# Other ranks for small transfers, and tiny vector operations planned freely, in the opening of an attention and two-MoE kernel

## The chip, the cores and the metric

The kernel runs on one core of one Trainium2 chip. The metric is the device time of one execution in microseconds (us); a comparison uses the median over several executions.

## What is computed

The reference chains three layers over 4 batches of 576 tokens.

```python
scores = scale * q @ k.T                      # 4 batches, 8 heads, 576 x 576, head size 64
cum = cumsum(maximum(s, 0))
bias = minimum(-(cum[:, None] - cum[None, :]), 0)
attn = softmax(where(causal, -1e9, scores + bias))
x = (attn @ v), heads side by side            # 2304 tokens x 512
x = moe(x, w_gate, w_val, w_out, rms_g)       # root-mean-square norm, silu(g) * val, 512 -> 1536 -> 512
x = moe2(x, w2_gate, w2_val, w2_out)          # the same without the norm
```

## The kernel before

All work is given to a planner as operations. Each has an engine, an assumed duration, the buffers that it reads and writes, and a rank `pri`. `Plan.run` walks an assumed timeline: when an engine comes free, it takes the ready operation with the lowest rank. The result is a fixed order of instructions for each engine. On the chip each engine (PE for matmuls, DVE, ACT, POOL, and SP, which only issues transfers) works through its own order and stands still where the next instruction's data has not come.

Two more inputs of an operation matter here. `later` adds nanoseconds to the time at which the planner believes that an operation's forerunners on compute engines have released it. `port` says that a DVE operation must not be planned while a POOL operation runs: the planner then puts it after that operation (`if e == POOL or e == DVE and ops[n][7]` in `Plan.run`).

The opening works on the first 256 rows of batches 0 and 1, 16 early heads in all (`EarlyUnit`, called u0 to u15 here, in the order in which they are planned). Head u has rank u, its loads have u - 1000. For each head three transfers are issued in `EarlyUnit.load`:

- L879: q and k of the head, 128 KB, into a slot of `lq` (`lq_117` for even heads, `lq_121` for odd ones, two slots in each);
- L884: one row of the cumulated s, 1 KB, into row 64 of the same slot, from the fifth head on. Below it is called the s row;
- L891: v of the head, 64 KB, into a slot of `vl` (four slots as well). The first four heads take it from ACT's queue.

The score matmul (L899) needs q, k and the s row; the values matmul (L927) needs v and the exponentials, which come through DVE (L690), ACT (L701), a transpose on PE (L917) and a copy (L923 on DVE or L922 on ACT). A slot is free for head u + 4 when PE is done with head u.

The weights of the first MoE layer come beside this: 24 weight loads of 512 KB (L434, tile `raw`, ranks -992 and up in steps of 1.5 for two), each turned into two parts by L438 on ACT, L440 on DVE, L445 or L446 on ACT or POOL, and L449 on POOL or DVE. When the eight heads of a batch are done, `normalise` (called with `split=False` for the early heads) runs a chain of some 20 tiny DVE operations on 128x2 and 128x16 values (L1020 to L1054, written through `step`), then transposes (L1058), matmuls (L1066) and scalings (L1070), and with that the MoE matmuls (L1086) of the batch can start. They are queued behind the attention as work that fills PE's gaps; the hidden values that they give are stored by L1126. The loads of the later attention (L597, L599, L602, L605, L774) go through SP too.

Of the kernel before, what the change touches and what calls it, by code (L numbers as in the profile page):

```python
# [40 lines left out]
PE, DVE, ACT, POOL, SP, NONE = "PE", "DVE", "ACT", "POOL", "SP", "NONE"  # L41


def f32(ap):
    return ap.bitcast(F32)
# [34 lines left out]
class Plan:  # L80
# [20 lines left out]
    def op(self, eng, ns, fn, r=(), w=(), pri=0.0, later=0, port=False, slow=0.0):  # L101

        n = len(self.ops)
        done = 0
        if eng == SP:  # L110
            took = ns / self.RATE
            ns = max(450.0, took)
            done = 2300.0 + took - ns + slow
        deps, shared = set(), []
        for accesses, writes in ((r, False), (w, True)):
            for a in accesses:
                buf, part = a if isinstance(a, tuple) else (a, None)
                key = buf if isinstance(buf, str) else buf.key
                live = self.live.setdefault(key, [])
                keep = []  # L120
                for part2, m, wrote in live:
                    meets = part is None or part2 is None or part == part2
                    if meets and (writes or wrote) and m != n:
                        deps.add(m)
                    if not (writes and meets and (part is None or part == part2)):
                        keep.append((part2, m, wrote))
                keep.append((part, n, writes))
                self.live[key] = keep
                if not isinstance(buf, str) and buf.share is not None and buf not in shared:
                    shared.append(buf)  # L130
                    buf.uses += 1
        engs = eng if isinstance(eng, list) else [(eng, ns)]
        self.ops.append((engs, fn, deps, pri, done, shared, later, port))
        return n
# [160 lines left out]
TINY = 70  # L295
# [5 lines left out]
def tile_kernel(  # L301
# [16 lines left out]
    op = plan.op  # L318
# [10 lines left out]
    def buf(pool, tag, shape, dtype, name=None):  # L329
        return Buf(f"{pool}.{tag}",  # L330
                   lambda: pools[pool][1].tile(shape, dtype, name=name or tag, tag=tag))
# [143 lines left out]
    cumA = buf("at", "pTB1", [P, 2 * P], F32, "cumA")  # L475
# [100 lines left out]
    class Head:  # L576
# [13 lines left out]
        def load(self, pri):  # L590
            b, h, n, nv = self.b, self.h, self.n, self.nv
            i = b * NH + h
            c0 = self.c0
            q0, k0, c0_ = lq_parts(self.ql, 0)
            q1, k1, c1_ = lq_parts(self.ql, 1)
            self.qp, self.kp = [k0, k1], [q0, q1, c0_, c1_]
            op(SP, 4 * P * n, lambda en: en.dma_start(  # L597
                out=self.ql()[:, :n], in_=qk[b, h, :, 1, :n]), w=self.kp, pri=pri, later=2500)
            op(SP, 4 * D * (QW - c0), lambda en: en.dma_start(  # L599
                out=self.ql()[:D, S + c0:], in_=qk[b, h, :D, 0, c0:]),  # L600
               w=self.qp, pri=pri, later=2500)
            op(SP, 4 * P * n, lambda en: en.dma_start(  # L602
                out=self.cb()[:, :n], in_=cum_d[i:i + 1, :n].to_broadcast([P, n])),
               r=["cum_d"], w=[self.cb], pri=pri, later=2500)
            op(SP, 256 * P * nv, lambda en: en.dma_start(out=self.vl()[:, :nv], in_=vp[b, h, :, :nv]),  # L605
               w=[self.vl], pri=pri, later=2500)
# [241 lines left out]
    class EarlyUnit(Unit):  # L848
# [28 lines left out]
        def load(self, pri):  # L877
            ql, i = self.ql
            op(SP, 8 * D * 256, lambda en: en.dma_start(  # L879
                out=ql()[0:D, :, 288 * i:288 * i + 256], in_=qk[self.b, self.h, 0:D, :, 0:256]),  # L880
               w=self.parts[:2], pri=pri)
            n = self.b * NH + self.h
            if not self.first:
                op(SP, 1024, lambda en: en.dma_start(  # L884
                    out=ql()[D:D + 1, 1, 288 * i:288 * i + 256], in_=cumA()[n:n + 1]),
                   r=[cumA, self.rows], w=self.parts[2:], pri=pri, later=1000)
            if self.first:
                op(ACT, 450, lambda en: en.dma_start(
                    out=self.v(), in_=vp[self.b, self.h, :, 0:2]), w=[self.vl], pri=pri - 1e6)
            else:  # L890
                op(SP, 512 * P, lambda en: en.dma_start(  # L891
                    out=self.v(), in_=vp[self.b, self.h, :, 0:2]), w=[self.vl], pri=pri)

        def scores(self, pri):
            for t in self.tiles:
# [44 lines left out]
    def normalise(i, g, tot, pri, split=True):  # L940
# [15 lines left out]
        for k in range(KD):  # L956
# [3 lines left out]
               r=[(x, (k, 0)), (x, (k, 64))], w=[q], pri=pri)  # L960

            if not split:
                def sums(en, q=q, k=k):
# [9 lines left out]
                    out=qh()[:, :n], in0=q()[:, :n], scalar1=1.0, scalar2=1.0, op0=ALU.mult,  # L973
                    op1=ALU.mult)}, r=[q], w=[qh], pri=pri)
            op([(DVE, c_tt(n)), (POOL, c_ptt(n))], 0, lambda en, q=q, qh=qh: en.tensor_tensor(
                out=sqL()[:, :n], in0=q()[:, :n], in1=f32(qh()[:, :n]),
                op=ALU.subtract), r=[q, qh], w=[sqL], pri=pri, port=True)
# [6 lines left out]
        if split:  # L984
# [3 lines left out]
               r=[ps], w=[sq[0]], pri=pri)  # L988
            ps2 = mo_bank()
            for c in range(nt):  # L990
                op(PE, C_TR, lambda en, c=c: en.transpose(
                    ps2()[:, c * P:c * P + P], sq[0]()[:, at[c]:at[c] + P], ident()),
                   r=[sq[0], ident], w=[ps2], pri=pri)
# [3 lines left out]

        def step(fn, r=(), w=None):
            w = [col] if w is None else w
            op(DVE, TINY, fn, r=[*w, *r], w=w, pri=pri, port=True)  # L1000

        def m():
            return col()[:, 0, :nt]
# [10 lines left out]
        def over():  # L1014
            return fac()[:, 0, :nt]

        def u():
            return fac()[:, 1, :nt]
        F, U = (fac, 0), (fac, 1)
        step(lambda en: en.tensor_scalar(out=over(), in0=tot()[:, :nt], scalar1=1.0e-9,  # L1020
                                         scalar2=None, op0=ALU.add), [tot], [F])
        step(lambda en: en.reciprocal(over(), over()), [], [F])
        step(lambda en: en.tensor_tensor(out=u(), in0=squares(), in1=over(), op=ALU.mult),
             [ps, F], [U])
        step(lambda en: en.tensor_tensor(out=u(), in0=u(), in1=over(), op=ALU.mult), [F], [U])
        step(lambda en: en.tensor_reduce(out=m(), in_=u(), axis=mybir.AxisListType.X,
                                         op=ALU.add), [U])
# [6 lines left out]
        for _ in range(3):  # L1034
# [6 lines left out]
            out=over(), in0=over(),  # L1041
            in1=y().rearrange("p (t o) -> p t o", o=1).to_broadcast([P, nt, NH]),
            op=ALU.mult), [col], [F])
# [7 lines left out]
        def columns(z):  # L1051
# [3 lines left out]
                                         op=ALU.subtract), [F], [rr])  # L1055
        tp = mo_bank()
        for c in range(nt):
            op(PE, C_TR, lambda en, c=c: en.transpose(  # L1058
                tp()[:, at[c]:at[c] + P], rr()[:, c * P:c * P + P], ident()), r=[rr, ident], w=[tp],
               pri=pri)  # L1060
        op(ACT, c_act(n), lambda en: en.activation(rT(), tp()[:, :n], ACTF.Copy),
           r=[tp], w=[last], pri=pri)
        for k in range(KD):
# [7 lines left out]
                out=x()[:, k, :n], in0=x()[:, k, :n], scalar=gcol()[:, k:k + 1], in1=rs()[:, :n],  # L1071
                op0=ALU.mult, op1=ALU.mult), r=[rs, gcol], w=halves, pri=pri)
            op(ACT, c_act(n) + 35, lambda en, k=k: en.activation(H()[:, k, :n], x()[:, k, :n], ACTF.Copy),  # L1073
               r=halves, w=[(H, k)], pri=pri)
            op([(POOL, c_ptt(n)), (DVE, c_tt(n))], 0, lambda en, k=k: en.tensor_tensor(  # L1075
                out=L()[:, k, :n], in0=x()[:, k, :n], in1=f32(H()[:, k, :n]), op=ALU.subtract),
               r=halves + [(H, k)], w=[(L, k)], pri=pri, port=True)
# [56 lines left out]
    later = setup()  # L1134
# [767 lines left out]
```

## Time and profile before

| | |
|---|---|
| median of 3 runs | 1056.55 us (1052.65 to 1058.98) |
| the profiled execution, its own time | 1057.39 us |
| its span, first to last instruction | 1055.6 us |
| PE busy | 1040.2 us, 99% of the span |
| mean granted TensorE clock | 0.997 of full speed |

The span leaves out 1.79 us around the first and last instruction. Busy time of PE counts a matmul from its start to its modelled end, so neighbours overlap, and a PE that runs at half clock is as busy as one at full clock.

### The profile page before, as it was taken

To read this page: it belongs to the slowest core of one execution; us is meant where nothing else is said; L and a number is where in the kernel's file an instruction comes from. 1 tells how busy PE (TensorE), PEld (TensorE's weight loads), DVE (VectorE), ACT (ScalarE), POOL (GpSimd) and SP (SyncE) were. 2 spreads that over 40 slices of the span, in tenths; PEclk is the share of its full clock that TensorE was granted. 3 is DMA by queue.
4 is the path that set the end of the run, shared out by engine and by line. 5 is a ranking of instruction groups with operands and counts; after the bars stand their busy time and mean duration, and the time that the engine had idled before them with its cause. 6 is when DMAs were issued, how large, how long until landed. Compare 5 with 4: busy or idle time off the path is not lost.

```text
span 1055.6 us, 19496 instructions
## 1 busy us (share of the span) xinstructions
PE 1040.2 (99%) x6322; PEld 937.2 (89%) x6322; DVE 771.7 (73%) x1880; ACT 641.5 (61%) x1373; POOL 273.5 (26%) x370
## 2 busy tenths in 40 slices
PE   8899999999999999999999999999999999999998
PEld 6599999999999999999988889888888888888888
DVE  7699788777777776757779887665667766976462
ACT  6689778867664775333466865555556444665652
POOL 4368556544343542000000000212122221300000
PEclk9899999999999999999999999999999999999999
DMA  7797555534546732666697662666667667888673
GB/s 204 229 282 221 144 150 148 164 117 128 158 142 204 246 106 85 188 208 206 206 299 244 197 222 84 222 210 220 228 202 256 219 232 263 292 259 261 207 244 105
DMA packets 127959, 211.17 MB, mean 200 GB/s; under 512 B 16176, under 2 KB 55600, under 8 KB 127856
## 3 DMA queue, kind: packets, MB, share of 16 engines
q1 hardware_dynamic: 126656, 209.32, 62.8%
q8 instruction: 50, 0.82, 0.3%
q10 hardware_dynamic: 1200, 0.60, 0.2%
q14 instruction: 53, 0.43, 0.1%
HBM read 145.29 MB, written 64.56 MB: 199 GB/s over the span
## 4 chain that ended last, share of the span: by engine, by line
PE 79%; DMA 7%; DVE 6%; ACT 3%; issue 3%; POOL 1%; SPq 1%; ACTq 0%; POOLq 0%; DVEq 0%
PE mo L1086 21%; PE mo L1455 8%; PE mo L1626 8%; PE sps L1626 6%; PE tp L1455 6%; PE sps L1455 5%; PE tp L745 4%; PE tp L733 3%; PE sps L664 2%; PE mo L1702 2%; DMA raw<-in_w_gv 2%; PE sps L1086 2%; PE tp L1086 2%; PE mo L1510 2%; DMA lq<-cumA 1%
## 5 line engine op out<-in xcount | busy, mean ns | idle before, releaser
L1086 PE MATMUL mo<-xL,H 128*128 128x256 f32 (+1 forms) x672 | 201.8, 300 | 0.1
L1086 PE MATMUL mo<-xH,H 128*128 128x256 f32 (+1 forms) x672 | 200.7, 300 | 0.3
L1086 PE MATMUL mo<-xH,L 128*128 128x256 f32 (+1 forms) x672 | 200.2, 298 | 0.0
L1351 DVE TENSOR_TENSOR hL<-hh,hH 128x512 fp32r<-128x512 f32 (+1 forms) x192 | 125.2, 662 | 67.1 <-ACT hH L1348 66.4
L1348 ACT ACTIVATE hH<-hh 128x512 fp32r<-128x512 f32 (+1 forms) x192 | 115.2, 603 | 91.6 <-DVE hL L1351 21.3
L1086 PEld LDWEIGHTS mo<-xL,H 128*128 128x128 f32 x672 | 127.0, 189 | 1.0 <-POOL xL L1075 0.5
L1086 PEld LDWEIGHTS mo<-xH,H 128*128 128x128 f32 x672 | 126.7, 189 | 1.1 <-ACT xH L1073 0.6
L1086 PEld LDWEIGHTS mo<-xH,L 128*128 128x128 f32 x672 | 126.9, 189 | 0.2
L701 ACT ACTIVATE sc<-sc,col 128x128 f32<-128x128 f32 (+3 forms) x128 | 73.2, 572 | 48.4 <-DVE col L690 46.1
L1455 PE MATMUL mo<-hH,wo 128*128 128x512 f32 x312 | 97.8, 389 | 0.0
L1455 PEld LDWEIGHTS mo<-hH,wo 128*128 128x128 f32 x312 | 58.6, 188 | 12.2
L1455 PE MATMUL mo<-hL,wo 128*128 128x512 f32 x156 | 61.1, 391 | 0.2 <-DVE hL L1351 0.2
L1455 PE MATMUL tp<-hH,wo 128*128 128x512 f32 x192 | 60.4, 389 | 0.0
L1093 ACT ACTIVATE t<-mo 128x256 f32<-128x256 f32 (+1 forms) x84 | 33.9, 403 | 43.4 <-PE mo L1086 43.3
L1632 ACT ACTIVATE u<-sps 128x512 f32<-128x512 f32 x48 | 28.5, 593 | 50.6 <-PE sps L1626 48.8
L745 PE MATMUL tp<-pTB,vst 128*128 128x320 f32 (+2 forms) x320 | 52.2, 294 | 1.6 <-ACT pTB L736 1.0
L1455 PE MATMUL sps<-hH,wo 128*128 128x512 f32 x168 | 52.9, 389 | 0.0
L1095 DVE SCALAR_TENSOR_TENSOR t<-t,mo 128x256 f32<-128x256 f32 (+1 forms) x84 | 37.8, 450 | 19.4 <-ACT t L1093 19.1
L738 DVE TENSOR_TENSOR pTB<-tp,pTB 128x512 fp32r<-128x512 f32 x64 | 44.0, 687 | 8.3 <-ACT pTB L736 7.2
L745 PEld LDWEIGHTS tp<-pTB,vst 128*128 128x128 f32 x320 | 46.5, 189 | 3.6 <-ACT pTB L736 1.7
L1589 POOL TENSOR_TENSOR tmp<-x,x 128x512 f32<-128x512 f32 x2 | 2.9, 1454 | 178.5 <-DVE x L1471 178.5
L733 PE MATMUL tp<-ident,sc 128*128 128x128 f32 x304 | 46.9, 274 | 0.6 <-DVE x L754 0.4
(289 smaller groups left out, 2925.9 us busy)
## 6 DMA issues: line engine op xcount, KB each, us to landing
raw<-in_w_gv SPq DMA_DIRECT2D x44, 511.8 KB, 5.4
tb<-h_d SPq DMA_DIRECT2D x48, 256.0 KB, 3.9
t<-tb SPq DMA_DIRECT2D x48, 256.0 KB, 2.4
hh<-t SPq DMA_DIRECT2D x48, 256.0 KB, 3.1
lq<-in_qk SPq DMA_DIRECT2D x32, 288.0 KB, 3.6
cb<-cum_d SPq DMA_DIRECT2D x32, 288.0 KB, 3.9
hh<-h_d SPq DMA_DIRECT2D x36, 256.0 KB, 3.6
h_d<-hh SPq DMA_DIRECT2D x54, 128.0 KB, 2.3
```

The lines of the kernel that those rows point to most:

```text
L701: op(ACT, c_act(o + m, 2) + 35, lambda en: en.activation(sc()[:m, :o + m], sc()[:m, :o + m], ACTF.Exp, scale=-1.0, bias=col()[:m, 0, t:t + 1],
L733: op(PE, C_TR, lambda en, pt=pt, a=a, kb=kb, t=t: en.transpose(pt()[:, a * P:a * P + P], self.sc[t]()[:, kb * P:kb * P + P], ident()), r=[ ...
L738: op(DVE, c_tt(n), lambda en, pt=pt, c=c: en.tensor_tensor(out=place(L, c), in0=source(pt, c), in1=f32(place(H, c)), op=ALU.subtract), r=[ ...
L745: op(PE, c_mm(n), lambda en, w=w, z=z, kb=kb, d0=d0, n=n, o=o: en.matmul(po()[:, o:o + n], vst[j]()[:, kb, :], pT[g][z]()[:, d0:d0 + n], s ...
L1086: op(PE, c_mm(n), lambda en, a=a, x=x, c=c, k=k, i=i: en.matmul(ps()[:, :n], a()[:, c], x()[:, k, :n], start=(k == 0 and i == 0), stop=(k ...
L1093: op(ACT, c_act(n), lambda en: en.activation(t()[:, :n], gp()[:, :n], ACTF.Tanh, scale=0.5), r=[gp], w=[t], pri=pri)
L1095: op(DVE, c_tt(n), lambda en: en.scalar_tensor_tensor(out=t()[:, :n], in0=t()[:, :n], scalar=1.0, in1=gp()[:, :n], op0=ALU.add, op1=ALU.mu ...
L1348: op(ACT, c_act(n) + 35, lambda en: en.activation(H(), src(), ACTF.Copy), r=[src, *after], w=[H], pri=pri)
L1351: lambda en: en.tensor_tensor(out=L(), in0=src(), in1=f32(H()), op=ALU.subtract),
L1455: op(PE, c_mm(n), lambda en, m=m, w=w, xx=xx, kk=kk, i=i: en.matmul(ps[m]()[:, :n], w(), xx(), start=first and kk == 0 and i == 0, stop=kk ...
L1626: op(PE, c_mm(n), lambda en, w=w, xx=xx, cut=cut, kk=kk, i=i: en.matmul(ps()[:, :n], W[w]()[:, cut], xx(), start=first and kk == 0 and i == 0,
L1632: op(ACT, c_act(n), lambda en: en.activation(dst(), ps()[:, :n], ACTF.Copy), r=[ps], w=[dst], pri=-1.0e4)
```

## The change

Three edits. The s rows of the early heads get a rank that is 3 lower, so that they go ahead of the q, k and v transfers and of the weight loads that stand near them. The v transfers of the early heads get a rank that is 2.2 higher and `later=800`, which puts them behind the q and k transfers of the next two heads. The tiny operations of the early `normalise` are planned without regard to POOL.

```diff
--- before.py
+++ after.py
@@ -883,13 +883,13 @@
             if not self.first:
                 op(SP, 1024, lambda en: en.dma_start(
                     out=ql()[D:D + 1, 1, 288 * i:288 * i + 256], in_=cumA()[n:n + 1]),
-                   r=[cumA, self.rows], w=self.parts[2:], pri=pri, later=1000)
+                   r=[cumA, self.rows], w=self.parts[2:], pri=pri - 3, later=1000)
             if self.first:
                 op(ACT, 450, lambda en: en.dma_start(
                     out=self.v(), in_=vp[self.b, self.h, :, 0:2]), w=[self.vl], pri=pri - 1e6)
             else:
                 op(SP, 512 * P, lambda en: en.dma_start(
-                    out=self.v(), in_=vp[self.b, self.h, :, 0:2]), w=[self.vl], pri=pri)
+                    out=self.v(), in_=vp[self.b, self.h, :, 0:2]), w=[self.vl], pri=pri + 2.2, later=800)
 
         def scores(self, pri):
             for t in self.tiles:
@@ -997,7 +997,7 @@
 
         def step(fn, r=(), w=None):
             w = [col] if w is None else w
-            op(DVE, TINY, fn, r=[*w, *r], w=w, pri=pri, port=True)
+            op(DVE, TINY, fn, r=[*w, *r], w=w, pri=pri, port=split)
 
         def m():
             return col()[:, 0, :nt]
```

Since ranks and assumed times feed the planner, the order of all engines changes from there on, to the end of the program. Names in the rows below carry the number of the tile; `raw_455` of before and `raw_449` of the change are the same weight load.

SP's order around the transfers of u13, before. `raw` is a weight load, `lq<-in_qk` q and k, `lq<-cumA` an s row, `vl` v; in turn they belong to u12 (s row), a weight load, u11 (v), a weight load, u13 (q and k), u12 (v), u13 (s row), u14 (q and k, s row), u13 (v), a weight load, u14 (v).

```order
L884 DMA lq_117<-cumA 1x16x16
L434 DMA raw_455<-in_w_gv 128x2047
L891 DMA vl_136<-in_vp 128x128
L434 DMA raw_479<-in_w_gv 128x2047
L879 DMA lq_121<-in_qk 64x2x256
L891 DMA vl_126<-in_vp 128x128
L884 DMA lq_121<-cumA 1x16x16
L879 DMA lq_117<-in_qk 64x2x256
L884 DMA lq_117<-cumA 1x16x16
L891 DMA vl_136<-in_vp 128x128
L434 DMA raw_543<-in_w_gv 128x2047
L891 DMA vl_126<-in_vp 128x128
```

The same place with the change: the s row of u12, a weight load, v of u10, the s row of u13, a weight load, the s row of u14, q and k of u13, v of u11, q and k of u14, a weight load, the s row of u15, a weight load.

```order
L884 DMA lq_117<-cumA 1x16x16
L434 DMA raw_449<-in_w_gv 128x2047
L891 DMA vl_126<-in_vp 128x128
L884 DMA lq_121<-cumA 1x16x16
L434 DMA raw_478<-in_w_gv 128x2047
L884 DMA lq_117<-cumA 1x16x16
L879 DMA lq_121<-in_qk 64x2x256
L891 DMA vl_136<-in_vp 128x128
L879 DMA lq_117<-in_qk 64x2x256
L434 DMA raw_527<-in_w_gv 128x2047
L884 DMA lq_121<-cumA 1x16x16
L434 DMA raw_557<-in_w_gv 128x2047
```

The s row of u13 has moved from behind both weight loads to between them; q and k of u13 stay behind both; v of u12, u13 and u14 have moved out of this stretch, and v of u10, which stood just ahead of it, has moved in.

SP's order where the last two v transfers of the early heads stand, before: q and k, the s row and v of u15, two weight loads, and the first loads of the later attention.

```order
L879 DMA lq_121<-in_qk 64x2x256
L884 DMA lq_121<-cumA 1x16x16
L891 DMA vl_136<-in_vp 128x128
L434 DMA raw_614<-in_w_gv 128x2047
L434 DMA raw_627<-in_w_gv 128x2047
L597 DMA lq_650<-in_qk 128x576
L599 DMA lq_650<-in_qk 64x384
L602 DMA cb_675<-cum_d 128x576
```

With the change v of u15 stands in the row before the last here, behind loads of the later attention and behind the store of the first hidden values (`h_d<-hh`).

```order
L434 DMA raw_701<-in_w_gv 128x2047
L434 DMA raw_725<-in_w_gv 128x2047
L597 DMA lq_747<-in_qk 128x576
L599 DMA lq_747<-in_qk 64x384
L602 DMA cb_768<-cum_d 128x576
L1126 DMA h_d_70<-hh_752 128x256
L605 DMA vl_789<-in_vp 128x320
L774 DMA cb_798<-cum_d 64x448 x2
L891 DMA vl_136<-in_vp 128x128
L434 DMA raw_821<-in_w_gv 128x2047
```

So v of u15 went from ahead of the weight loads `raw_614` and `raw_627` to behind these two (now `raw_612` and `raw_636`), two more, the first loads of the later attention, and a store that waits for DVE's result of the first MoE matmuls; v of u14 went to the row just ahead of `raw_701`.

PE's order around the first score matmul of u13 (`sps_564`), before. It follows the scores of u12 (`sps_537`), the values of u10 (`tp_548`) and the transposes of u11 (`tp_557`).

```order
L899 MATMUL sps_537<-lq_117 128x256
L927 MATMUL tp_548<-pTA_223,vl_126 64x256
L927 MATMUL tp_548<-pTA_223,vl_126 64x128
L917 MATMUL tp_557<-ident,sc_510 128x128
L917 MATMUL tp_557<-ident,sc_515 128x128 x2
L899 MATMUL sps_564<-lq_121 128x128
L965 MATMUL mo_569<-half,sq_334 128x2 x2
L899 MATMUL sps_575<-lq_121 128x256
```

With the change, where u13's first score matmul is `sps_546`:

```order
L899 MATMUL sps_537<-lq_117 128x256
L899 MATMUL sps_546<-lq_121 128x128
L927 MATMUL tp_550<-pTA_223,vl_126 64x256
L927 MATMUL tp_550<-pTA_223,vl_126 64x128
L917 MATMUL tp_561<-ident,sc_510 128x128
L917 MATMUL tp_561<-ident,sc_515 128x128 x2
L965 MATMUL mo_570<-half,sq_333 128x2 x2
L899 MATMUL sps_577<-lq_121 128x256
L899 MATMUL sps_583<-lq_117 128x128
```

It has moved ahead of the values of u10, and the scores of u14 (`sps_583`) have come up behind it.

## Rows read from the trace of the kernel before

**Rows 1.** The page, busy time: an engine, then groups (busy us, mean ns).

```profile
PE 1040.2 (99%) x6322; PEld 937.2 (89%) x6322; DVE 771.7 (73%) x1880; ACT 641.5 (61%) x1373; POOL 273.5 (26%) x370
...
L1093 ACT ACTIVATE t<-mo 128x256 f32<-128x256 f32 (+1 forms) x84 | 33.9, 403 | 43.4 <-PE mo L1086 43.3
...
L1095 DVE SCALAR_TENSOR_TENSOR t<-t,mo 128x256 f32<-128x256 f32 (+1 forms) x84 | 37.8, 450 | 19.4 <-ACT t L1093 19.1
```

**Rows 2.** Busy time of each engine by stretches, with PE's granted clock.

```profile
core 0: us, PE busy (x) PEld busy (x) DVE busy (x) ACT busy (x) POOL busy (x), PEclk, DMA share, GB/s
...
14.00:35.80 21.80, 21.21 (x122) 14.39 (x122) 17.58 (x69) 18.46 (x58) 8.72 (x9) 1.00 0.67 183
35.80:38.30 2.50, 0.03 (x1) 0.02 (x1) 0.63 (x2) 1.22 (x3) 1.48 (x2) 1.00 0.67 205
38.30:45.10 6.80, 6.79 (x21) 4.49 (x22) 2.67 (x12) 2.08 (x8) 1.94 (x2) 0.50 0.53 154
45.10:52.00 6.90, 6.07 (x38) 4.34 (x36) 6.15 (x19) 5.76 (x16) 2.39 (x2) 1.00 0.99 344
...
60.00:100.00 40.00, 39.35 (x309) 38.22 (x309) 38.01 (x125) 35.27 (x83) 32.62 (x40) 1.00 0.80 252
100.00:200.00 100.00, 99.92 (x784) 98.70 (x783) 79.89 (x283) 78.12 (x198) 59.24 (x94) 1.00 0.54 154
200.00:400.00 200.00, 197.55 (x1464) 193.44 (x1463) 152.31 (x529) 133.30 (x342) 86.38 (x138) 1.00 0.51 157
400.00:1000.00 600.00, 599.12 (x3186) 522.04 (x3186) 431.56 (x745) 328.91 (x587) 72.00 (x62) 1.00 0.68 219
```

**Rows 3.** PE in order of time (start us, duration; in brackets idle time before, ended by).

```profile
14.07 0.46 PE L899 MATMUL sps<-lq 128*128 128x128 f32 x2 [1.05 <-DMA lq<-cumA]
...
34.49 0.86 PE L927 MATMUL tp<-pTA,vl 128*64 128x256 f32 x4 [0.21 <-ACT pTA L922]
...
38.31 0.77 PE L899 MATMUL sps<-lq 128*128 128x128 f32 x2 [2.48 <-DMA lq<-cumA]
...
46.68 0.86 PE L927 MATMUL tp<-pTA,vl 128*64 128x256 f32 x4 [0.65 <-DVE pTA L923]
```

**Rows 4.** The chain that ended last, 28 to 40 us (start us, duration).

```profile
31.70 6.48 DMA lq<-cumA
```

**Rows 5.** SP's issues in order of time, 16 to 44 us.

```profile
17.03 0.58 SPq L486 DMA_DIRECT2D gcol<-in_rms_g  x1
...
18.31 0.53 SPq L891 DMA_DIRECT2D vl<-in_vp  x1
18.88 0.43 SPq L434 DMA_DIRECT2D raw<-in_w_gv  x1
...
26.60 1.56 SPq L891 DMA_DIRECT2D vl<-in_vp  x1
...
28.82 0.57 SPq L434 DMA_DIRECT2D raw<-in_w_gv  x1
...
37.04 0.33 SPq L891 DMA_DIRECT2D vl<-in_vp  x1
```

**Rows 6.** Issue to landing: weight loads of 28.82 and 29.91, q/k of 30.38.

```profile
DMA to landing us min/median/max: 4.1/4.1/4.1
...
DMA to landing us min/median/max: 7.1/7.1/7.1
...
DMA to landing us min/median/max: 7.3/7.3/7.3
```

**Rows 7.** Issue to landing of the 12 v transfers of L891.

```profile
DMA to landing us min/median/max: 1.8/4.2/6.6
```

**Rows 8.** ACT in order of time: a weight load's first operation.

```profile
37.00 0.77 ACT L438 ACTIVATE cvy<-raw 128x512 f16<-128x512 bf16 x1 [1.65 <-DMA raw<-in_w_gv]
```

**Rows 9.** POOL: two L449 in order of time, and three of 40 to 60 us.

```profile
21.37 3.11 POOL L449 TENSOR_TENSOR L<-raw,H 128x512 fp32r<-128x512 f32 x2
...
L449 POOL TENSOR_TENSOR L<-raw,H 128x512 fp32r<-128x512 f32 x3 | 3.9, 1298 | 5.7 <-ACT H L445 5.6
```

## The prediction

> **What bounds the kernel now.** First the busy times: PE is busy for 1040.2 of 1055.6 us [rows 1], so all that any change of order can win lies in PE's idle time and in what makes its matmuls long. The second view, busy time by stretches, says where [rows 2]. From 100 to 1000 us PE is idle for 0.08 + 2.45 + 0.88 = 3.4 us in all; from 60 to 100 us for 0.65 us, although DVE is at 95% there. In the opening, two stretches stand out: 35.8 to 38.3 us, where PE does nothing, and 38.3 to 45.1 us, where it is busy throughout, but at a granted clock of 0.50 (1.2 GHz). In the third view, PE in order of time, the idle stretch is one wait of 2.48 us, of the first score matmul of u13 for an s row [rows 3]. The chain names the same transfer: issued at 31.70, landed 6.48 us later, at 38.18 [rows 4].
>
> What the s row stands behind is read from SP's issues and their landings. The weight load of 29.91 landed after 7.1 us, at 37.0; q and k of u13, issued at 30.38, after 7.3 us, at 37.7 [rows 5, 6]. So of u13's wait, q and k explain all but the last 0.5 us. SP itself also stood still: the v transfer at 37.04 is the eighth issue behind the weight load of 29.91, and went when that had landed [rows 5, 6]. I read this as at most eight transfers of SP in flight.
>
> The slow clock follows the wait. At half clock 6.8 us of matmuls are 3.4 us of work at full clock, so the wait has cost 2.48 + 3.4 = 5.9 us, if PE sets the pace there. It does: DVE is busy for 2.67 and ACT for 2.08 of these 6.8 us [rows 2]. An earlier wait, of 1.05 us up to 14.07, left the clock at 1.00 [rows 2, 3].
>
> **The change part by part.** *The s row of u13* is issued between the two weight loads. Alone this is worth the 0.5 us by which it came after q and k.
>
> *The weight loads come earlier.* In the new order the transfer of `gcol` at 17.03 and the v transfer at 18.31 are behind the weight load of 18.88: two issue slots of 0.63 and 0.57 us, 1.2 us. The v transfer at 26.60, whose issue took 1.56 us, is behind the load of 28.82 [rows 5]. The two loads ahead of q and k of u13 can thus start 1.2 to 2.8 us earlier, and DMA has room: its share was 0.67 from 14 to 35.8 us [rows 2]. q and k cannot be issued before PE has finished u10's scores, about as before. They land 0.7 us behind the second load, as before: at 34.9 to 36.5. As bound below nothing of that, 37.7; as bound above, both loads land 4.1 us after issue like the first one did into an emptier queue [rows 6], and q and k are there before they are needed.
>
> *PE needs them earlier too.* u13's scores now stand ahead of u10's values, so they are due at 34.49 - 0.21 = 34.3, not at 35.8 [rows 3]. The wait is then between 0 and 3.4 us; from the middle of the shift, some 0.6 to 2.2 us. I take 0.9, near the lower end, since the v transfers that shared the engines in that stretch are gone. It is below the 1.05 us that the clock stood. Won: 2.48 - 0.9 = 1.6 us, and the clock's 3.4 us.
>
> *The tiny operations.* They are some 20 instructions either way, on a DVE that was idle for much of 35.8 to 45.1 us [rows 2]. In DVE's order the last of them stood behind u13's and u14's work; now they are through before u13's second scores. In PE's order the MoE matmuls of batch 0 now start before the values of u13 to u15, and give PE work while those are late. What this adds is the wait of 0.65 us for DVE at 46.68 [rows 3], which may or may not go; I take 0.3.
>
> *The v transfers behind.* In PE's order the values of u12 to u15 stand later too, so nothing waits in the likely case, and SP no longer stands before weight loads waiting for a slot of v. The price is on ACT: its order holds the first operation of each weight load, and a late one stops it, as at 37.00 for 1.65 us [rows 8]. PE will run some 5 us ahead of before, the loads only by the 1.2 to 2.8 us above. Bounds 0 and 1.65 us; I take 0.6, towards the lower one, since v no longer holds SP up ahead of the later loads.
>
> *The rest of the program* is put in another order with the same matmuls. Only the 3.4 us above are in play; nothing favours either sign, and I take 0 with 1.5 us each way.
>
> Sum: -1.6 - 3.4 - 0.3 + 0.6 = -4.7 us against the profiled execution's 1057.39, that is 1052.7. That execution lies 0.8 us above the median of the runs, 1056.55. I split that difference and predict 1052.3. A measurement of this kernel tells about 0.5%, 5.3 us, from no change, so the forecast itself lies just inside that.
>
> **The rivals.** *The wait stays (the change does not do what it says).* q and k of u13 stand behind both weight loads as before. If the loads gain only the lower 1.2 us, the wait is 36.5 - 34.3 = 2.2 us, and the clock falls again, as it did after 2.48: 0.3 us won there, 0.3 for DVE, 0.6 lost, 1057.4, and 1056 to 1058 with the rest's spread. For it: 7.1 us for a load under the same crowding. Against: three v transfers fewer.
>
> *A new wait takes its place, and the kernel is slower.* v of u15 is now issued behind the first store of hidden values. In PE's order 48 MoE matmuls, 4 score matmuls and the 4 of u14's values lie between the matmuls that this store waits for and the matmul that needs v of u15: 56 at 0.127 us (99.92 / 784, [rows 2]), 7.1 us. Of these 0.40 + 2 x 0.45 = 1.3 us go to the store's forerunners [rows 1], and four issues of some 0.45 us lie between: v has 4.0 us to land. Its transfers took 1.8 to 6.6, median 4.2 [rows 7]. At 6.6 PE waits 2.6 us and the clock falls for another 3.4: 1052.7 + 6.0 = 1058.7, slower. It decides from a landing at which the clock falls, somewhere between 5.1 and 6.5 us (waits of 1.05 and 2.48). Against it: SP stands still before that store, so the queue drains and v should land in 2 to 3 us.
>
> *The tiny operations meet POOL.* Two of POOL's subtractions took 3.11 us together, three others 1.298 each [rows 9]; so one was held up by 0.5 us, where DVE worked beside it. If three of the steps are held for a whole one of 1.3 us, and the next scores behind them, 3.9 of the 4.7 us are gone: 1056.6. POOL had work for only 1.48 + 1.94 of the 9.3 us from 35.8 to 45.1 [rows 2], so three is much. The Trainium skill, SBUF — State Buffer, section "Who interferes with whom", says that a DVE instruction with two inputs in SBUF and a GpSimd instruction that reads SBUF exclude each other, and that the one that came second waits for the whole of the other. By that rule the hits would be few, but each as long as the operation met; the trace shows one lengthening of the kind, and none by a whole operation.
>
> **How the numbers follow.** The forecast has 0.62: 1048.5 to 1055.5 by its own bounds (no wait and no loss on ACT give -6.7; a wait of 1.7 with the clock held and 1.65 on ACT give -2.9; the rest adds 1.5 each way). The wait that stays has 0.18, the wait for v of u15 0.12, POOL 0.08. Over 5.3 us below the median is under 1051.3: 0.38, all from the forecast. Over 5.3 us above is over 1061.8: 0.06, from the wait for v where it comes with a late q and k or a poor later order. The rest, 0.56, is within. A range from 1047.5 to 1058.5 leaves out some 0.1 on either side.
>
> **What would show it right or wrong.** Right: PE's wait before u13's scores under 1.1 us, the clock at 1.00 from 14 to 60 us, the weight load that stood at 28.82 issued by 27.6, the MoE matmuls of batch 0 starting by 46 us, and idle time from 100 to 1000 us within 1.5 of 3.4 us. Wrong: a stretch at 0.50 anywhere before 60 us, an idle PE before a values matmul (L927) that waits for `vl`, ACT waiting over 1.65 us in all for `raw`, or POOL's L449 at 2 us and more. If all steps hold and the time still does not move, the later order has eaten it.

## The result: slower by 1%, and the profile after

The changed kernel takes 1066.03 us in the median (7 runs, 1061.16 to 1070.67) against 1055.3 us of the kernel before on the same chip: a ratio of 1.0104, with a 95% interval of 1.0071 to 1.0136. The forecast was 1052.3 us, the range 1047.5 to 1058.5. The profiled span is 1068.1 us against 1055.6.

The first view is the busy time by stretches, as in [rows 2].

```profile
core 0: us, PE busy (x) PEld busy (x) DVE busy (x) ACT busy (x) POOL busy (x), PEclk, DMA share, GB/s
...
14.00:35.80 21.80, 19.50 (x113) 13.06 (x111) 18.14 (x70) 18.69 (x61) 8.57 (x9) 1.00 0.69 186
35.80:38.30 2.50, 1.84 (x6) 1.26 (x6) 0.00 (x0) 0.17 (x2) 1.10 (x1) 0.61 0.98 313
38.30:45.10 6.80, 6.71 (x30) 4.86 (x28) 3.56 (x16) 3.72 (x12) 1.94 (x2) 0.64 0.60 196
...
60.00:100.00 40.00, 37.24 (x270) 36.02 (x268) 37.65 (x113) 31.53 (x74) 26.34 (x32) 0.91 0.73 226
100.00:200.00 100.00, 97.57 (x759) 95.51 (x757) 84.35 (x279) 76.63 (x192) 57.73 (x88) 1.00 0.56 156
200.00:400.00 200.00, 196.06 (x1436) 191.50 (x1437) 155.53 (x530) 130.71 (x337) 83.46 (x134) 0.99 0.54 159
400.00:1000.00 600.00, 597.49 (x3206) 522.26 (x3205) 433.00 (x766) 331.21 (x600) 72.17 (x63) 1.00 0.66 216
```

There is still a stretch at a granted clock of 0.50, from 36.3 to 43.2 us. There is a second one between 60 and 100 us (clock 0.91 in the mean, PE idle for 2.76 us), and from 100 to 1000 us PE is idle for 2.43 + 3.94 + 2.51 = 8.9 us, where it was idle for 3.4. PE in order of time, at its three longest waits from 30 to 100 us:

```profile
36.46 0.55 PE L899 MATMUL sps<-lq 128*128 128x128 f32 x1 [2.59 <-DMA lq<-in_qk]
...
73.17 0.41 PE L664 MATMUL sps<-kHH,qst 128*128 128x384 f32 x1 [2.07 <-DVE col L690]
...
74.68 0.58 PE L664 MATMUL sps<-kHH,qst 128*128 128x288 f32 x1 [0.69 <-DVE rc L1037]
```

The wait of u13 is as long as before [rows 3]; only its releaser has another name, q and k instead of the s row. SP's issues show why (behind them the landing of q and k, and then that of the two weight loads):

```profile
27.08 0.58 SPq L434 DMA_DIRECT2D raw<-in_w_gv  x1
...
28.84 0.57 SPq L434 DMA_DIRECT2D raw<-in_w_gv  x1
...
30.05 0.59 SPq L879 DMA_DIRECT2D lq<-in_qk  x1
```

```profile
DMA to landing us min/median/max: 6.3/6.3/6.3
```

```profile
DMA to landing us min/median/max: 3.9/5.3/6.6
```

The loads did go 1.1 to 1.7 us earlier, but q and k of u13 are still issued behind both, and land 0.9 us behind the second (28.84 + 6.6 = 35.4; 30.05 + 6.3 = 36.3). They came 1.3 us earlier than before; PE came there 1.9 us earlier (36.46 - 2.59 = 33.9 against 38.31 - 2.48 = 35.8).

The second wait is DVE's. First DVE in order of time, then POOL, in the changed kernel:

```profile
68.60 0.63 DVE L1028 TENSOR_SCALAR rc<-rc 128x2 f32<-128x2 f32 x1
69.26 0.17 DVE L1030 TENSOR_SCALAR rc<-rc 128x2 int32<-128x2 int32 x1
69.47 1.27 DVE L1032 TENSOR_SCALAR rc<-rc 128x2 int32<-128x2 int32 x1
70.78 0.78 DVE L1035 SCALAR_TENSOR_TENSOR rc<-rc 128x2 f32<-128x2 f32 x1
71.48 0.68 DVE L440 SCALAR_TENSOR_TENSOR raw<-raw,cvy 128x512 uint32<-128x512 uint32 x1
...
72.15 0.41 DVE L690 CUSTOM_DVE_ANT_0 sc<-sps,cb 128x256 f32<-128x256 f32 x1
```

```profile
68.19 1.01 POOL L616 TENSOR_TENSOR qst<-lq,qst 64x384 fp32r<-64x384 f32 x1
69.28 1.43 POOL L619 TENSOR_TENSOR kLL<-lq,kHH 128x576 fp32r<-128x576 f32 x1
70.68 0.86 POOL L628 TENSOR_TENSOR vst<-vl,vst 128x320 fp32r<-128x320 f32 x1
```

These are tiny steps of batch 1's normalise. Undisturbed ones take 0.15 to 0.17 us; here three take 0.63, 1.27 and 0.78 us, and each ends 0.02 to 0.03 us behind a subtraction of POOL (69.23 and 69.20, 70.74 and 70.71, 71.56 and 71.54). Behind them in DVE's order stands L690, which empties the bank that PE needs for its next scores: so PE stood for 2.07 us. From 73.9 to 80.7 us its granted clock was 0.50.

### The profile page after: what moved, and what is told of

Read it like the earlier page. It is cut to its first block, busy times and chain, and to the rows that moved or that the text cites. A ratio compares the mean times of both kernels' runs of the same rounds, so it can differ in the third digit from the quotient of the medians.

```text
span 1068.1 us, 19471 instructions
## 1 busy us (share of the span) xinstructions
PE 1046.9 (98%) x6322; PEld 943.0 (88%) x6322; DVE 787.8 (74%) x1888; ACT 642.8 (60%) x1377; POOL 265.2 (25%) x358
## 4 chain that ended last, share of the span: by engine, by line
PE 52%; DVE 5%; DMA 5%; ACT 2%; issue 1%; SPq 0%; ACTq 0%; DVEq 0%
PE mo L1626 9%; PE mo L1086 8%; PE sps L1626 8%; PE mo L1455 7%; PE tp L1455 4%; PE sps L1455 3%; PE mo L1702 3%; PE sps L1086 2%; PE mo L1510 2%; PE tp L1086 2%; PE tp L1626 1%; DVE hL L1351 1%; DMA hh<-t 1%; DMA hh<-h_d 1%; ACT hH L1348 1%
## 5 line engine op out<-in xcount | busy, mean ns | idle before, releaser
L1455 PEld LDWEIGHTS mo<-hH,wo 128*128 128x128 f32 x312 | 58.6, 188 | 12.1
L1093 ACT ACTIVATE t<-mo 128x256 f32<-128x256 f32 (+1 forms) x84 | 34.0, 405 | 45.1 <-PE mo L1086 40.1
L738 DVE TENSOR_TENSOR pTB<-tp,pTB 128x512 fp32r<-128x512 f32 x64 | 43.7, 686 | 13.5 <-ACT pTB L736 12.8
L1095 DVE SCALAR_TENSOR_TENSOR t<-t,mo 128x256 f32<-128x256 f32 (+1 forms) x84 | 37.7, 449 | 18.3 <-ACT t L1093 17.6
L619 POOL TENSOR_TENSOR kLL<-lq,kHH 128x576 fp32r<-128x576 f32 x28 | 42.0, 1500 | 29.1 <-ACT kHH L612 26.3
```

The costliest lines, as they stand in the source:

```text
L619: op([(POOL, c_ptt(n)), (DVE, c_tt(n))], 0, lambda en: en.tensor_tensor(out=kl()[:, :n], in0=ql()[:, :n], in1=f32(kh()[:, :n]), op=ALU.sub ...
L738: op(DVE, c_tt(n), lambda en, pt=pt, c=c: en.tensor_tensor(out=place(L, c), in0=source(pt, c), in1=f32(place(H, c)), op=ALU.subtract), r=[ ...
L1093: op(ACT, c_act(n), lambda en: en.activation(t()[:, :n], gp()[:, :n], ACTF.Tanh, scale=0.5), r=[gp], w=[t], pri=pri)
L1095: op(DVE, c_tt(n), lambda en: en.scalar_tensor_tensor(out=t()[:, :n], in0=t()[:, :n], scalar=1.0, in1=gp()[:, :n], op0=ALU.add, op1=ALU.mu ...
L1455: op(PE, c_mm(n), lambda en, m=m, w=w, xx=xx, kk=kk, i=i: en.matmul(ps[m]()[:, :n], w(), xx(), start=first and kk == 0 and i == 0, stop=kk ...
```

## How the runs were read

For each run I worked out a **loss**: the start of the PE matmul that has w us of work ahead of it, minus w. The work of a matmul is the median distance to the next start for its shape and tiles in the kernel before, so it is the same in all runs, whatever the order. The loss holds idle time and slow matmuls alike. At 80 us of work it is 14.7 us in the kernel before and 17.8 in the changed one; from there to 1020 us of work it grows by another 12.3 us and 21.6 us. So of the 12.5 us between these two spans, 3.1 are lost in the opening and 9.3 behind it. Each ratio is to the kernel before on the same chip; each loss is that of one profiled execution.

| run | ratio, 95% interval | loss to 80 us | loss behind |
|---|---|---|---|
| kernel before | 1 | 14.7 | 12.3 |
| changed kernel | 1.0104 (1.0071 to 1.0136) | 17.8 | 21.6 |
| *order of before behind the cut:* | | | |
| D1 s to 60 | 1.0010 (0.9992 to 1.0028) | 12.7 | 12.9 |
| D2 v to 60 | 1.0058 (1.0032 to 1.0083) | 19.6 | 12.6 |
| D3 tiny operations to 60 | 1.0040 (1.0024 to 1.0057) | 17.4 | 12.8 |
| D4 s and v to 60 | 1.0030 (1.0011 to 1.0049) | 16.0 | 10.0 |
| A1 all three to 60 | 1.0077 (1.0047 to 1.0107) | 24.9 | 11.4 |
| B2 all three to 45 | 1.0056 (1.0035 to 1.0077) | 17.0 | 11.3 |
| B3 all three and q/k to 45 | 1.0010 (0.9992 to 1.0028) | 13.6 | 11.9 |
| C1 s and q/k to 45 | 0.9985 (0.9968 to 1.0002) | 13.8 | 12.5 |
| *all planned anew:* | | | |
| A3 tiny operations | 1.0066 (1.0043 to 1.0089) | 13.9 | 17.6 |
| A4 v | 1.0099 (1.0071 to 1.0128) | 16.1 | 19.3 |
| B4 s | 1.0066 (1.0040 to 1.0092) | 14.0 | 16.3 |
| C2 s and q/k | 1.0048 (1.0029 to 1.0066) | 15.2 | 12.7 |
| B1 no edit, one estimate lower | 1.0061 (1.0035 to 1.0087) | 12.7 | 16.8 |
| C3 no edit, the same one higher | 1.0023 (1.0003 to 1.0044) | 8.6 | 15.5 |
| A2 before to 60, then changed | 1.0079 (1.0051 to 1.0108) | 17.9 | 18.4 |
| C4 changed, xL on POOL | 1.0073 (1.0047 to 1.0099) | 20.7 | 14.7 |

The loss of an opening scatters widely from one execution to the next. At 60 us of work, up to about where the order is the same on all engines, the opening of before had lost 13.6, 14.5, 11.6 and 8.0 us in four executions (kernel before, A2, B1, C3), and the changed one 15.8, 20.0 and 17.7 us in three (changed kernel, A1, C4). One source of this is the wait of u4's first scores near 14 us: 1.05, 2.56, 1.85 and 0.95 us in the first four, 0.28, 3.38 and 1.89 us in the other three. So the 3.1 us above lie within the scatter, and what an opening costs is read from the ratios.

## The experiments

**Two orders in one program.** Both plans are made, then the operations that one starts before a cut on its planner's clock, then all others in the order and on the engines of the other. No operation changes. Only an operation whose buffer is still taken at the seam waits for it.

```
first, rest = plans[OPENING], plans[1 - OPENING]
out = [(n, e) for t, _, n, e in first if t < CUT]
done = {n for n, _ in out}
out += [(n, e) for _, _, n, e in rest if n not in done]
```

**A1 and A2.** `OPENING, CUT = 1, 60000.0` (the changed kernel first) and `0, 60000.0` (that of before first).

> Both kernels' orders are planned, and the program is issued in the changed kernel's order as far as its planner's clock runs to 60 us (its first 305 PE operations, which on the chip end at 59.5 us), and from there in the order of the kernel before. Theory A (late order): the edits themselves cost little in the first 60 us, and the loss comes with the order that the planner then makes of the rest; so the time is that of the kernel before within 2 us, 1053 to 1058, with u13's wait of 2.6 us and its stretch at 0.50 still there, but no wait of 2 us near 73 us. Theory B (opening): batch 1's normalise, 6 us later on the chip, leaves work on DVE that is owed behind, whatever the order; then the time stays at 1062 to 1067.

> The reverse: the order of the kernel before as far as the planner's clock runs to 60 us (its first 297 PE operations, 60.3 us on the chip), then the changed kernel's order. Theory A (late order): 1062 to 1068, the changed kernel's loss kept, though none of its edits stands in what is issued first. Theory B (opening): 1053 to 1058.

Measured: 1064.3 us and 1063.2 us. Neither theory holds alone; each half costs by itself. By the losses the order behind does what theory A says of it (11.4 with that of before, 18.4 with the changed one), but the opening costs as well, which theory A denied: in A1 PE waits for DVE for 2.08, 0.66 and 1.51 us between 77 and 82 us. The two prices do not add up: 0.77% and 0.79% alone, 1.04% together.

**A3, A4, B4: each edit alone,** as in the diff, with everything planned anew.

> Only the tiny operations' edit (they are not held back from POOL), s rows and v transfers as before. Theory A (late order): the opening to 45 us is that of the kernel before, but the rest is planned anew, so the time moves by several us either way, with waits of PE that stand at 70 to 600 us; 1055 to 1066, and no telling from the edit. Theory T (the tiny operations meet POOL and hold DVE): it has most of the loss by itself, 1062 to 1067, in lengthened tiny operations.

> Only the v transfers' edit. Theory A (late order): planned anew as well, 1055 to 1066, idle time of PE spread over 70 to 600 us. Theory V (the values of u14 and u15 and with them batch 1's normalise come late, which costs PE 5 us by 80 us): 1060 to 1066, with a second wait of 2 us and a second stretch at 0.50 near 73 us; and without it, if the tiny operations or the s row are the cause, about 1055.

> Only the s rows' edit. Theory A: planned anew like the others, 1057 to 1064. Theory E (each edit has its own price, and this one removes the wait): 1049 to 1054. Theory D says of the opening that u13's wait stays at 2 us and more, for q and k, and the clock falls behind it.

Measured: 1061.16, 1064.87 and 1061.59 us. Each is slower, and each loses 16.3 to 19.3 us behind the opening. That fits theory A, but doesn't tell an edit's own price from that of planning anew. The second wait that theory V gave A4 near 73 us did not come. In B4 u13 waited for q and k as theory D says, but for 1.55 us and with the clock left at 1.00, where it gave 2 us and a slow stretch.

**B1 and C3: no edit at all,** but the planner's estimate for the exponentials of one head of the second stage.

```
-            op(ACT, c_act(o + m, 2) + 35, lambda en: en.activation(
+            op(ACT, c_act(o + m, 2) + (15 if len(units) == 20 else 35), lambda en: en.activation(
```

C3 has 55 in place of 15.

> The kernel before with none of the three edits: only the planner's estimate for the exponentials of one head of the second stage is 20 ns lower (15 for 35 in its constant). PE's first 469 operations (to 83 us on the chip) keep their order, all behind is planned anew; POOL gets 354 operations where the kernel before has 372 and the changed one 360. Theory A (the order behind the opening is worse however it is disturbed): 8.5 us more were lost behind the first 60 us of work in the run with the order of before first and that of the changed kernel behind, so this one too is at 1058 to 1064, with an opening as before. Theory E (it is the edits): as before, 1051 to 1056.

> The estimate for the exponentials of the same head as before, but 20 ns higher (55 for 35) instead of lower; no other edit. Theory A: 1058 to 1064 again, since the order behind 82 us is again another one. If the lower estimate's loss was that one order's bad luck: this one is as likely below the kernel before as above it, 1050 to 1058.

Measured: 1060.09 us and 1057.14 us. Twenty ns in one estimate, with PE's order unchanged to some 82 us, cost 0.61% and 0.23%; both intervals lie above 1, that of C3 barely. C3 is 0.9 us short of what theory A gave it and inside the range of its rival (one order's bad luck), so by its time alone it does not decide between them. Its loss behind, 15.5, is still above that of every run with the old order there (10.0 to 12.9). These two also carry the old opening, and so show what it does in other executions. PE at u13's wait in B1, and in C3:

```profile
38.41 0.46 PE L899 MATMUL sps<-lq 128*128 128x128 f32 x2 [0.49 <-DMA lq<-cumA]
```

```profile
35.91 0.46 PE L899 MATMUL sps<-lq 128*128 128x128 f32 x2 [0.39 <-DMA lq<-cumA]
```

With A2's 1.77 and the 2.48 of [rows 3], one and the same order waited there for 0.39 to 2.48 us. C3 had no stretch at 0.50 before 300 us.

**B2 and B3: the changed opening to 45 us,** `OPENING, CUT = 1, 45000.0`; B3 also with

```
-               w=self.parts[:2], pri=pri)
+               w=self.parts[:2], pri=pri,
+               alt=None if self.first else (pri - 3, 0, False))
```

(`alt` is the rank, `later` and `port` of the plan that comes first).

> The changed kernel's order only as far as its planner's clock runs to 45 us (its first 195 PE operations, 44 us on the chip), then that of before. Theory C (two costs: the changed order of 45 to 80 us, in which the MoE matmuls start before batch 1's normalise, some 5 us; and the order behind, some 7 us): both are gone here, so 1051 to 1056. If the cost lies in what the three edits do before 44 us, it stays at 1059 to 1065.

> As the run before it, and q and k of the early heads are ranked 3 ahead as their s rows are, so that those of u12 and u13 are issued ahead of the second of the two weight loads. Theory D (u13's wait and the half clock behind it come from q and k behind both loads, not from the s row): the wait is under 1.1 us, no stretch at 0.50, and 4 to 6 us are won against the kernel before, 1047 to 1051. Rival: the weight load that is now later, or another transfer, is waited for in its place: 1052 to 1057.

Measured: 1060.18 us and 1055.95 us. Theory C falls with B2: the order up to 45 us alone brings 0.56% of A1's 0.77%, though in part by waits that come behind the cut. In B3 u13's wait is gone (0.21 us are left; PE waits for 0.45 us at u14's, for DVE) and there is no half clock behind it, as theory D says, but it is no faster than before. PE in order of time shows the rival, v:

```profile
49.95 0.62 PE L1003 MATMUL tp<-pTA,vl 128*64 128x256 f32 x2 [0.41 <-DMA vl<-in_vp]
...
55.95 0.84 PE L1003 MATMUL tp<-pTA,vl 128*64 128x256 f32 x4 [1.12 <-DMA vl<-in_vp]
...
58.05 0.49 PE L1041 MATMUL mo<-half,sq 128*128 128x2 f32 x3 [1.26 <-ACT sq L1034]
```

(In programs of two orders the lines stand 73 to 76 lower: L1003 is L927, L1041 is L965.) The values wait for v, and the squares of batch 1's normalise for the values: 2.8 us. B2 has the same pair, 1.50 and 1.26 us.

**C1 and C2: without the v edit.** The s rows and q and k 3 ahead, v and tiny operations as before; C1 to 45 us and then in the old order, C2 planned anew.

> Of the edits only the s rows', and q and k of the early heads ranked 3 ahead too, in the order as far as the planner's clock runs to 45 us; then the order of before. v transfers and tiny operations as before. Theory V (behind the v edit stand the waits for v of 0.4 and 1.1 us at 50 and 56 us, and one of 1.3 us behind them, in the run with all edits and q and k first): these are gone, the wait of u13 too, and 3 to 5 us are won: 1049 to 1053. Rival (a late weight load or the seam at 45 us costs it): 1055 to 1058.

> The same two edits of ranks, but with the order that the planner makes of all the rest. Theory A (the order behind the opening is worse whenever it is planned anew, 4 to 9 us): the opening wins as in the run before it, and the rest gives it back and more: 1055 to 1061, 4 to 8 us above that run. Theory E (the edits decide): within 2 us of it.

Measured: 1054.01 us and 1060.73 us. The waits for v are gone and PE waits for 1.07 us before u13's scores in C1, at a clock of 1.00 to 1053 us; yet only 0.15% is won, the interval holds 1, and the time lies between the two forecasts. In two of the three other executions of the old order the wait that it removes was under 0.5 us, so there were hardly 3 to 5 us to win. The same two edits planned anew are 6.7 us above that; this is theory A's prediction, though C2's profiled execution lost little behind the opening (12.7) and does not show where.

**C4: what makes the new orders slower behind.** The changed kernel, with one operation bound to POOL.

```
-            op([(POOL, c_ptt(n)), (DVE, c_tt(n))], 0, lambda en, k=k: en.tensor_tensor(
+            op(POOL, c_ptt(n), lambda en, k=k: en.tensor_tensor(
                 out=L()[:, k, :n], in0=x()[:, k, :n], in1=f32(H()[:, k, :n]), op=ALU.subtract),
```

> The changed kernel, and the subtractions of normalise that make xL (L1075) on POOL alone; the planner gave DVE 14 of them in the changed kernel. POOL gets 378 operations instead of 360. Theory F (what the new orders lose behind the opening is DVE's: its operations that POOL holds up, 11 to 14 us of lengthening from 80 to 340 us instead of 6 to 7, and the subtractions that it took over from POOL): 3 to 6 us are won against the changed kernel, 1060 to 1063, with DVE's busy time from 80 to 340 us back at 245 to 248 us. Rival (the order, not the share of the engines): 1064 to 1068 all the same.

Measured: 1063.53 us. DVE's instructions from 80 to 340 us sum to 245.8 us, as expected (252.5 in the changed kernel; they overlap, so the windows below show less), and the loss behind is 14.7 instead of 21.6; the opening, with waits for DMA of 1.89 and 2.48 us, took 3 of these back. The time is 0.5 us above theory F's range and below the rival's, and its interval overlaps that of the changed kernel, so the gain itself is not shown. What speaks for theory F is DVE's load. Busy time from 80 to 340 us in the kernel before, then in the changed one, in B1, and in C2:

```profile
80.00:340.00 260.00, 257.35 (x1928) 252.12 (x1927) 205.86 (x713) 187.00 (x472) 134.88 (x211) 1.00 0.53 156
```

```profile
80.00:340.00 260.00, 255.69 (x1886) 249.61 (x1886) 212.27 (x711) 187.59 (x472) 131.34 (x201) 0.99 0.54 155
```

```profile
80.00:340.00 260.00, 255.37 (x1899) 248.83 (x1898) 212.97 (x712) 184.94 (x469) 122.21 (x196) 1.00 0.50 150
```

```profile
80.00:340.00 260.00, 258.31 (x1934) 253.16 (x1933) 215.08 (x729) 189.23 (x479) 125.61 (x197) 1.00 0.52 156
```

Third and fifth engine: DVE is busy for 6 to 9 us longer in the new orders, and POOL has 196 to 201 operations instead of 211. Of these, 3 to 6 us are lengthening (each DVE duration minus the lower quartile of its shape over all runs, summed: 7.2 us before, then 12.8, 12.1 and 10.4). By the same measure all nine runs with the old order behind the opening have some 6 to 7 us of lengthening, and the nine others 10 to 15 us, C4 among them, with DVE's sum back at 245.8. C2 is the case against: as much load on DVE, and little lost in its profile. So DVE's load and the lengthening go with the new orders, but are a part of the cause at most; which waits a new order will have, the load alone doesn't tell.

**D1 to D4: each edit's own price,** in the first 60 us, with the old order behind: `OPENING, CUT = 1, 60000.0`, and `alt` at that edit's line alone.

> Only the s rows' edit, in the order as far as the planner's clock runs to 60 us, then the order of before. Theory V (the opening's price is the v edit's): no loss, 1052 to 1056. Theory G (the seam at 60 us costs several us whatever stands before it): 1058 to 1062.

> Only the v transfers' edit, to 60 us, then the order of before. Theory V: most of the 8 us of the run with all three edits to 60 us, so 1058 to 1062, with PE waiting for v or for what the late values hold up (squares of normalise, L958 and L965) between 45 and 65 us. Theory G: 1058 to 1062 as well, but waits only from 60 us on. Theory T (the tiny operations): 1052 to 1056.

> Only the tiny operations' edit, to 60 us, then the order of before. Theory V: 1052 to 1056. Theory T (they meet POOL's operations, and the scores behind them on DVE come late): 1057 to 1062, with lengthened steps of L1020 to L1054 and PE waiting for DVE.

> The edits of s rows and v transfers, to 60 us, then the order of before; tiny operations as before. Theory V: as with v alone, 1057 to 1062. If the wait of 2 us near 73 us in the changed kernel (and in the run with its order to 60 us, at 77) needs the tiny operations' edit, it is not here, and the time is 2 to 5 us under that run's 1064.

Measured: 1055.54, 1061.92, 1059.08 and 1058.59 us. The s rows cost nothing, and the seam behind them doesn't either, so theory G falls. v and the tiny operations each have a price, about 6 and 4 us; with the s rows' edit beside it (D4) v's is 3 us, and the intervals of D2 and D4 overlap. D3 shows the tiny operations' most plainly, DVE, then POOL, then PE:

```profile
60.30 0.83 DVE L1102 TENSOR_SCALAR rc<-rc 128x2 f32<-128x2 f32 x1
61.17 1.91 DVE L1104 TENSOR_SCALAR rc<-rc 128x2 int32<-128x2 int32 x1
63.11 0.17 DVE L1106 TENSOR_SCALAR rc<-rc 128x2 int32<-128x2 int32 x1
```

```profile
60.23 0.88 POOL L701 TENSOR_TENSOR vst<-vl,vst 128x320 fp32r<-128x320 f32 x1 [1.18 <-ACT vst L699]
61.06 0.23 POOL L855 TENSOR_SCALAR_AFFINE_SELECT sc<-cb 64x64 f32<-64x64 f32 x1
61.26 1.30 POOL L522 TENSOR_TENSOR L<-raw,H 128x512 fp32r<-128x512 f32 x1
62.52 0.53 POOL L751 TENSOR_SCALAR_AFFINE_SELECT sc<-cb 128x128 f32<-128x128 f32 x2
```

```profile
64.77 0.74 PE L862 MATMUL sps<-kHH,qst 128*128 128x448 f32 x1 [2.61 <-DVE col L763]
```

A step of 0.17 us took 1.91 us, until POOL's run of operations ended at 63.05; PE then waited for the scores' bank for 2.61 us, and the clock was 0.50 from 64.1 to 70.9. A3 has the same wait of 2.62 at 67.30, with no v edit either. D2 has one of 3.27 us at 77.58 although its tiny operations are held back: there the late v makes batch 1's normalise late, and its steps (0.91 and 1.32 us at 74.49 and 75.43) fall among POOL's subtractions for the second stage. D4, with s and v, has no such wait in its profile; but that is one of its shorter executions, 1056.39 us in a spread from 1054.22 to 1063.68.

## Why the prediction was wrong, point by point

- **The step that failed most** is "*The rest of the program* is put in another order with the same matmuls ... nothing favours either sign, and I take 0 with 1.5 us each way". The kernel before has an order that loses 10.0 to 12.9 us behind the opening in nine profiled runs; orders planned anew lose 12.7 to 21.6 in nine others. B1 and C3 price that by itself: 0.61% and 0.23%, 6.4 and 2.4 us, for an edit that is none. In the changed kernel's profile it is 9.3 us. In the medians it is A2 that shows it: the opening of before, the changed order behind, 0.79% or 8.3 us. So there was a favoured sign. Whether the order of before is simply the best of many that had been tried, no run here tells. The rest of the miss is the opening's, forecast at -4.7 us: it came to +3.1 us in the changed kernel's profile, and A1 prices it at 0.77%, 8.1 us.
- **The tiny operations** stood in the sum at -0.3, and as a rival at 3.9 us with a chance of 0.08. The mechanism was right and nearly the size (D3: 0.40%, 4.2 us), the place was not: I weighed it by POOL's work from 35.8 to 45.1 us, where batch 0's chain runs, and not by that of batch 1's chain, which runs in the stretch from 60 to 100 us, where POOL is busy for 32.62 of 40 us [rows 2]. The reading that the trace of before shows one lengthening of the kind, "and none by a whole operation", overlooked this chain. One of its steps there, and the operation of POOL with whose end it ended:

```profile
66.75 1.25 DVE L1028 TENSOR_SCALAR rc<-rc 128x2 f32<-128x2 f32 x1
```

```profile
66.54 1.43 POOL L619 TENSOR_TENSOR kLL<-lq,kHH 128x576 fp32r<-128x576 f32 x1
```

Six of the 18 steps of batch 1's chain took 0.41 to 1.25 us there, although they were planned around POOL, and PE waited for no more than 0.31 us at a time from 60 to 100 us. That chain was spread from 61.5 to 91.3 us; in the changed kernel it runs from 67.4 to 78.5, in D3 from 58.4 to 67.6. What was new is then less the hold than several holds close together, ahead of what PE needs next from DVE; this is argued from the traces, not tested. And two inputs in SBUF, the condition that the prediction quotes, are those of L1035 alone among the three held steps of the changed kernel: L1028 and L1032 have one.

- **The v transfers behind**: "nothing waits in the likely case". In the changed kernel itself v of u15 is there in time (issued at 55.9, landed 2.3 us later, needed at 60.5), so the rival of that wait didn't come true there; nor did ACT wait for a weight load at all. But v late costs 2.8 us in B2 and B3, and late values push batch 1's normalise among POOL's work (D2: 0.58%).
- **The wait of u13 and the clock**, -5.0 in a sum of -4.7: the rival in which the wait stays came true (q and k still behind both loads, 2.59 us and a stretch at 0.50). The reason for the low end, fewer v transfers beside the loads, did not hold: the second load took 6.6 us (7.1 before). In the four executions of the changed opening the wait was 2.59, 3.00, 2.06 and 2.48 us (changed kernel, A1, B2, C4), each with a slow stretch behind it; in four of the old one 2.48, 1.77, 0.49 and 0.39 us. So the change made this wait steadier and, if anything, longer. With q and k ahead of the second load it was 0.21, 1.07 and 0.95 us (B3, C1, C2), with no slow stretch behind it. But the term was mis-sized from the start: the one execution's 5.9 us was the dearest of the four, and C1, which removes the cost, wins 0.15%, not clear of nothing.
- **The weight loads** did come 1.1 to 1.7 us earlier, within my 1.2 to 2.8 but for 0.1, though not for both of its reasons: `gcol` is still issued ahead of the weight load that stood at 18.88 (14.22 and 16.75 us). Nor did u10's scores hold q and k of u13 back: the slot is that of u9, whose scores ended at 27.6 us before and 27.3 us after, and SP issued them in its turn at 30.4 and 30.1.
- **What was to show it wrong** did: a stretch at 0.50 before 60 us, and 8.9 us idle from 100 to 1000 us against 3.4 with 1.5 each way; the MoE matmuls of batch 0 started at 47.4 us, not by 46. The sign that I had named for the tiny operations, POOL's L449 at 2 us, did not show (1.83 at most): POOL held DVE's steps, not they POOL. The rivals had been priced one at a time and from the forecast; here two came together (the wait that stays, the tiny operations), with the later order's loss on top.
- **A slip in the sum of the bounds:** no wait and no loss on ACT give -2.48 - 3.4 - 0.3 = -6.2 us, not -6.7, which puts the forecast's lower bound at 1049.3. The miss is on the other side.

What stays open: why just these new orders meet more waits behind the opening, beyond the load on DVE; why the prices of A1 and A2 do not add up; and how much of D2's and D4's difference is chance.

## What to carry to other kernels

Where a planner sets the order, an edit of three ranks is an edit of the whole program: price that first, by a change of one estimate that means nothing, and keep the old order behind the edit when an edit is to be judged. A wait for a transfer is to be read in several executions before it is booked as a gain. A chain of tiny steps is to be laid against the other engine's work over the whole stretch where it runs, and for each chain of its kind.

## What the runs showed of the hardware

- One DVE step of 0.17 us was held for 1.91 us, through four POOL operations in a row (61.06 to 63.05 in D3). The Trainium skill, SBUF — State Buffer, section "Who interferes with whom", counts `tensor_scalar`, which this step is, among the DVE instructions that can contend with GpSimd, and has one instruction wait for the whole of the other; the trace agrees, and here the hold outlasted one operation and went on through those that followed it.
- A wait's length alone didn't decide on the clock. A PE wait of 1.70 us left the granted clock at 1.00 (C1 and D1, up to 14.7 and 14.0 us), and so did one of 2.26 us in C2, up to 15.3 us; 1.73 us in D2, up to 36.0, and 1.85 us in B1, up to 14.9, were followed by a stretch at 0.50 (1.2 GHz).
- The same transfers, issued in the same order, cost PE from 0.39 to 2.48 us before u13's scores and from 0.95 to 2.56 us before u4's, in four executions.
